# A fused attention, gated-layer and routed-expert kernel: the root's chain on another engine, values loaded earlier, and several pieces of work emitted in another order

## The chip, the cores and the metric

The kernel runs on one core of one Trainium2 chip. A core has a matmul engine (TensorE, "PE" in the rows; its weight loads are listed apart as "PEld"), VectorE ("DVE"), ScalarE ("ACT"), GpSimd ("POOL") and SyncE ("SP"), which issues most of the DMAs. Each engine works through its own list of instructions in order; semaphores make one engine wait for another. SBUF is the working memory, PSUM the memory into which TensorE writes (eight banks of 128 x 512 words of 32 bits). The metric is the device time of one execution in microseconds (us); a run's number is the median of several executions.

## The reference

Three layers follow each other. All inputs are 32-bit floats.

```python
# 1. attention with a sigmoid in place of the softmax: 4 batches, 12 heads, 448 tokens, 64 wide
scores = scale * (q @ k.T) - log(S)
attn_out = sigmoid(scores) @ v                     # laid side by side: x is 1792 x 768
# 2. a gated layer
xn = x / sqrt(mean(x * x) + 1e-6) * rms_g
g, val = xn @ w_gate, xn @ w_val                   # 768 -> 1536
x = (g * sigmoid(g) * val) @ w_out                 # 1536 -> 768
# 3. one of 8 experts for each token
e = argmax(x @ w_gate2); p = softmax(x @ w_gate2)[e]
out = p * (relu(x @ w1[e]) @ w2[e])                # 768 -> 1024 -> 768
```

## The kernel before

The program is one straight list per engine. Python generators emit it: one step emits a piece for each engine, and what one step emits stands in the engines' lists behind what the step before emitted. `later(n, f)` puts a piece off by n ticks.

**Attention.** The 12 heads of a batch make 6 pairs, so there are 24 pairs u over the 4 batches. A pair takes 3.5 steps on the average (two pairs share the rest of 64 tokens), 21 steps a batch (`QS`), 84 in all. Step t issues the scores of its part (`quarters`, L736, PSUM tiles `two`), the weighted sums of the part two steps back (`weighted`, L753, PSUM tiles `one`), and the sigmoid (`weights`, L742, on ScalarE). At a pair's first part SyncE loads the queries and keys of pair u + 2 (`load_pair`, tile `rqk`) and the values of pair u + 1 (`load_v`, tile `rv`). When a pair is summed up, ScalarE copies one PSUM bank, VectorE adds the other (L781), ScalarE squares, VectorE adds the squares to the batch's sum `ss` (L791).

**Beside the attention.** `normalise(b)` starts in the sixth step after batch b's last one: TensorE sums `ss` over the partitions (`pm`, L821), VectorE makes a first estimate of 1 / root (L825 to L833), then a chain of 12 small instructions (three Newton turns, L836 to L839, tiles `ta` and `ya`) refines it; ScalarE spreads it (`yb`, L843), TensorE turns it (`pr`, L847), and six VectorE instructions scale x (L852). One batch after another, the fourth within the gated layer. `conv` (`narrow`, L216 to L229) puts the gated layer's weights together from two halves of 64-bit words on VectorE and stores them to DRAM; SyncE loads the next words. The table `x_at` says in which step the operands of the first seven products are made (`x_sum` L332 and L335, `x_hi` L319, `x_lo` L323).

**Gated layer.** Two batches make a half p. Seven products stand for eight in each of 12 column groups n; `slot(p, n, k)` issues one product, nine matmuls, because each operand is a high and a low part and three of their four products are kept (`three`, L310 to L312). `window(p, n, k)` emits what ScalarE and VectorE do beside it. `abc` holds two sets of three PSUM banks that the column groups take in turn; `dup` (L369) copies one bank into another.

**Output.** `output(p)` has 6 output chunks of 8 turns. The list `pys` gives the bank of a sum. Beside the first turns stand the last window of the gated part (`window(p, KF, m)`) and the high and low parts of what it made (`h_hi`, `h_lo` L457).

**Routing and experts.** `route(b)` is a generator of small steps; half 1's gated part carries those of batches 0 and 1, the expert blocks those of 2 and 3 (`turn(b, steps)`, called by a table of block numbers). Its small matmuls write the bank `mi` (`pl` L592, `pn` L618, `pr` L636 and L637). A batch has 14 expert blocks, 8 of the first weight and 6 of the second. `split_block` makes the high and low part of a block's weight (ScalarE L918, VectorE L919). `mi_bank` takes the next bank of `fixed["mi"]`, which holds one bank, `mi`.

Of the kernel before, what the change touches and what calls it, by code (L numbers as in the profile page):

```python
# [91 lines left out]
def block_kernel(ctx, tc, qkp, v, wg, wv, wo, g, gate, w1, w2, consts, out):  # L92
# [404 lines left out]
    def output(p):  # L497
        pair = {}
        pys = [abc[1][i] for i in (1, 0, 2)]
        logit_bank[2 * p], logit_bank[2 * p + 1] = mi, one[2]  # L500
# [23 lines left out]
        for m in range(8 * KD):  # L524
            oc, q = divmod(m, 8)
            x, g = divmod(q, 4)
            if g == 0:
                pys.append(pys.pop(0))
                py = pys[-1][:, :S]
            h, l = out_w[oc, g // 2]  # L530
            xh, xl = held["hs", g, x, 0][0], held["hs", g, x, 1][0]
            for i in range(HALF):
                c = HALF * g + i
                three(py, (h[:, c % KD, :], l[:, c % KD, :]), (xh[:, i, :], xl[:, i, :]), c == 0, c == KF - 1)
            if oc == KD - 1:
                drop(("hs", g, x, 0))
                drop(("hs", g, x, 1))
            if g == 3:
                later(2, out_copy, py, oc, x)
                if x == 1:  # L540
                    logits(2 * p, oc)
                elif oc > 0:
                    logits(2 * p + 1, oc - 1)
            if m < 2:
                window(p, KF, m)
            if m < 4:
                h_hi(*((3, 0), (1, 1), (2, 1), (3, 1))[m])
            if 0 < m < 5:
                h_lo(*((3, 0), (1, 1), (2, 1), (3, 1))[m - 1])
            if oc + 1 < KD:  # L550
                if q in (0, 3):
                    load_raw(2 * NU * p + 2 * (KF + oc + 1) + q // 3)
                if q >= 4:
                    (hi_o, lo_o)[q % 2](p, oc + 1, q // 2 - 2)
            yield m
# [22 lines left out]
    def route(b):  # L578
# [82 lines left out]
        pf = sm([CT, NC], "pf")  # L661
        nc.vector.tensor_copy(out=pf, in_=ri[:, 1, :])
        for c in range(NC):
            j = b * NC + c
            nc.vector.tensor_scalar(
                out=p1_all[:, j, :],
                in0=const("place", CT),
                scalar1=pf[:, c : c + 1],
                scalar2=const("token1", CT)[:, j : j + 1],
                op0=ALU.is_equal,  # L670
                op1=ALU.mult,
            )
# [35 lines left out]
    def attention():  # L708
# [85 lines left out]
        load_v(0)  # L794
        load_pair(1)
        normal = iter(())
        for t in range(B * QS + LAG):
            if t < B * QS:
                u, c = order[t]
                if c == 0:  # L800
                    load_v(u + 1)
                    load_pair(u + 2)
                quarters(t)
# [13 lines left out]
    def normalise(b):  # L817
# [17 lines left out]
        for _ in range(3):  # L835
            nc.gpsimd.tensor_tensor(out=ta, in0=ya, in1=ya, op=ALU.mult)  # L836
            nc.gpsimd.tensor_tensor(out=ta, in0=ta, in1=va, op=ALU.mult)
            nc.gpsimd.tensor_scalar(out=ta, in0=ta, scalar1=1.5, scalar2=None, op0=ALU.add)
            nc.gpsimd.tensor_tensor(out=ya, in0=ya, in1=ta, op=ALU.mult)  # L839
        for _ in range(4):  # L840
            yield
        yb = keep.tile([CT, NC, 128], F32, tag="xr", name="yb")
        nc.scalar.copy(out=yb, in_=ya.unsqueeze(2).to_broadcast([CT, NC, 128]))  # L843
        yield
        pr = mi[:, :S]
# [284 lines left out]
    def all_slots():  # L1130
# [96 lines left out]
    x_at = {  # L1227
        43: [(x_hi, 0, P1, True)], 44: [(x_lo, 0, P1)], 46: [(x_hi, 0, P2, True)], 47: [(x_lo, 0, P2)],
        64: [(x_sum, 0, P5)], 65: [(x_sum, 0, P7)], 66: [(x_hi, 0, P5, True)], 67: [(x_lo, 0, P5)],
        68: [(x_sum, 0, P6)], 69: [(x_hi, 0, P6, True)], 70: [(x_lo, 0, P6)], 71: [(x_sum, 0, P4)],  # L1230
        72: [(x_hi, 0, P7, True)], 73: [(x_lo, 0, P7)],
    }
    end, done = B * QS, 0
    for n in range(end + LAG):
# [13 lines left out]
        for f, *a in x_at.get(n, ()):  # L1248
            f(*a)
        scaling = n >= QS and n % QS >= 15  # L1250
        if 2 <= n < 70 and not scaling and n not in (44, 47) and (n < 63 or n % 2 == 0):
            next(conv)
            done = (done + 1) % 3
        elif n == 72 and done:
            for _ in range(done, 3):
                next(conv)
# [11 lines left out]
        if n == end:  # L1268
# [3 lines left out]
            abc += [[one[0], *four_banks[:2]], [one[1], *four_banks[2:]]]  # L1272
            slot(0, -1, 4)
        if n == end + 1:
            s_a.close()
            s_x, xd = opened("xd", side="right", reuse_waits="tile")
            s_w, cw = opened("cw", side="right", reuse_waits="tile")
            for r in range(2, 6):
                load_raw(r)
            dup(0)  # L1280
            hi_w(0, 0, P7)
# [75 lines left out]

    fixed.update(mm=abc[0], sc=[abc[1][1], abc[1][0]], av=[abc[1][2], one[2]])
    s_m.close()
# [41 lines left out]
    for u, b, steps in (  # L1401
        (0, 2, 2), (1, 2, 2), (1, 3, 2), (2, 2, 2), (3, 2, 1), (3, 3, 2), (4, 3, 2), (5, 3, 2), (6, 3, 1)
    ):
# [34 lines left out]
    for u in range(B * NB):  # L1438
        if u % NB >= K2 - 1 and u % NB < NB - 1:
            split_block(u + 1)  # L1440
        out_of = block(u)
        tick()
        out_of()
        if (u + 2) % NB < K2:
            split_block(u + 2)
# [73 lines left out]
```

## Time and profile before

| | |
|---|---|
| median of 3 executions | 920.24 us (919.37 to 921.02) |
| the profiled execution, its own time | 919.88 us |
| its span, first to last instruction | 918.0 us, mean granted clock 0.992 |
| TensorE busy | 895.4 us, 98% of the span |
| VectorE busy | 598.3 us, 65% |
| ScalarE busy | 377.1 us, 41% |
| GpSimd busy | 32.0 us, 3% |
| chain that ended last | TensorE 86%, VectorE 7%, DMA 3% of the span |

The span is what the profile sees; about 1.9 us lie around it. TensorE's busy time is so near the span that the time is its work and the places where it waits or runs at half its clock; the views that list these places are the ones to read.

### The profile page before, as it was taken

The page shows a single profiled execution, that of the slowest core. Times are in us where ns is not written, and L with a number is a line of the kernel's source. Part 1 is how long each engine was busy: PE and PEld are TensorE (multiplying, and loading weights), DVE is VectorE, ACT ScalarE, POOL GpSimd, SP SyncE. Part 2 cuts the span into 40 slices and gives each one's busy share as a digit, 9 for nine tenths or more (in the row PEclk, how much of TensorE's full clock was granted, in tenths as well). Part 3 has the DMA queues.
Part 4 walks back from the last instruction along what each step waited for, and adds up shares of the span by engine and source line. Part 5 has one row for each costly group of instructions (what it writes and reads, how often), then busy time and mean ns, then how long its engine had stood idle before and what let it go on. Part 6 is the DMA issues. An engine that isn't in the chain of part 4 may idle for free.

```text
span 918.0 us, 14308 instructions
## 1 busy us (share of the span) xinstructions
PE 895.4 (98%) x5430; PEld 749.4 (82%) x5430; DVE 598.3 (65%) x1074; ACT 377.1 (41%) x605; POOL 32.0 (3%) x59
## 2 busy tenths in 40 slices
PE   8999989999999999999999999999989999999997
PEld 3445435999999889999899998999879988888996
DVE  3777676998988984777897778222576734334454
ACT  6778857444445512354444455121222222222230
POOL 0022040200000000000000000000000000000000
PEclk9999989999999999999999999999999999999999
DMA  8996763354445399841222242547747958749533
GB/s 327 392 347 230 277 215 130 117 202 152 142 138 172 114 330 318 240 114 37 70 69 70 91 150 82 151 131 217 213 112 241 318 181 293 256 149 300 166 61 62
DMA packets 118202, 169.33 MB, mean 184 GB/s; under 512 B 62233, under 2 KB 82585, under 8 KB 118128
## 3 DMA queue, kind: packets, MB, share of 16 engines
q1 hardware_dynamic: 104960, 164.85, 54.5%
q10 hardware_dynamic: 13024, 2.98, 1.7%
q8 instruction: 43, 0.70, 0.3%
q0 software_dynamic: 144, 0.53, 0.3%
q14 instruction: 31, 0.25, 0.1%
HBM read 127.57 MB, written 40.63 MB: 183 GB/s over the span
## 4 chain that ended last, share of the span: by engine, by line
PE 86%; DVE 7%; DMA 3%; POOL 1%; issue 1%; ACT 1%; SPq 0%; DVEq 0%; ACTq 0%; POOLq 0%
PE four L312 13%; PE four L311 13%; PE four L310 13%; PE one L310 12%; PE one L312 12%; PE one L311 12%; PE one L753 4%; PE two L736 4%; DVE m L457 1%; DMA w32d<-wn 1%; PE one L570 1%; DMA w<-in_wg 1%; DMA rv<-in_v 1%; DVE wc L286 1%; PE four L1097 1%
## 5 line engine op out<-in xcount | busy, mean ns | idle before, releaser
L312 PE MATMUL one<-m,wc 128*128 128x448 f32 x282 | 103.2, 366 | 0.0
L310 PE MATMUL one<-m,wc 128*128 128x448 f32 x282 | 102.6, 364 | 0.0
L311 PE MATMUL one<-m,wc 128*128 128x448 f32 x282 | 102.3, 363 | 0.0
L742 ACT ACTIVATE a<-two,logs 128x896 f32<-128x896 f32 x84 | 84.6, 1008 | 30.6 <-PE two L736 28.7
L736 PE MATMUL two<-rqk 64*64 64x448 f32 x672 | 90.4, 557 | 3.8 <-DMA rqk<-in_qkp 3.8
L753 PE MATMUL one<-a,rv 64*64 64x448 f32 x672 | 87.9, 542 | 1.3 <-DMA rv<-in_v 1.2
L312 PE MATMUL four<-m,wc 128*128 128x448 f32 x213 | 78.0, 366 | 0.7 <-DVE wc L286 0.7
L310 PE MATMUL four<-m,wc 128*128 128x448 f32 x213 | 77.6, 364 | 0.0
L311 PE MATMUL four<-m,wc 128*128 128x448 f32 x213 | 77.5, 364 | 0.0
L311 PE MATMUL four<-m,wr 128*128 128x448 f32 x192 | 70.3, 366 | 1.4 <-DVE m L457 1.4
L310 PE MATMUL four<-m,wr 128*128 128x448 f32 x192 | 69.8, 364 | 0.3 <-DVE m L437 0.3
L312 PE MATMUL four<-m,wr 128*128 128x448 f32 x192 | 69.8, 363 | 0.0
L286 DVE TENSOR_TENSOR wc<-raw,wc 128x384 fp32r<-128x384 f32 x115 | 61.6, 549 | 4.5 <-ACT wc L281 4.5
L736 PEld LDWEIGHTS two<-rqk 64*64 64x64 f32 x672 | 30.7, 137 | 39.3 <-issue 21.8
L753 PEld LDWEIGHTS one<-a,rv 64*64 64x64 f32 x672 | 31.0, 135 | 37.7 <-issue 30.7
L311 PEld LDWEIGHTS one<-m,wc 128*128 128x128 f32 x282 | 52.8, 187 | 4.6
L281 ACT CAST wc<-raw 128x384 fp32r<-128x384 f32 x115 | 55.0, 515 | 3.4 <-PE four L311 1.2
L310 PEld LDWEIGHTS one<-m,wc 128*128 128x128 f32 x282 | 52.9, 188 | 4.0
L312 PEld LDWEIGHTS one<-m,wc 128*128 128x128 f32 x282 | 52.9, 188 | 3.8
L918 ACT CAST w2h<-w2r 128x1024 fp32r<-128x1024 f32 x24 | 25.2, 1049 | 59.9 <-PE four L311 30.0
L310 PE MATMUL four<-xc,wr 128*128 128x448 f32 x126 | 47.4, 376 | 0.0
L311 PE MATMUL four<-xc,wr 128*128 128x448 f32 x126 | 46.8, 371 | 0.0
(253 smaller groups left out, 1895.3 us busy)
## 6 DMA issues: line engine op xcount, KB each, us to landing
raw<-w32d SPq DMA_DIRECT2D x70, 384.0 KB, 3.6
w32d<-wn SPq DMA_DIRECT2D x36, 384.0 KB, 3.2
w1r<-in_w SPq DMA_DIRECT2D x24, 512.0 KB, 6.1
w2r<-in_w SPq DMA_DIRECT2D x32, 384.0 KB, 6.4
x2s<-x SPq DMA_DIRECT2D x48, 224.0 KB, 2.0
rqk<-in_qkp SPq DMA_DIRECT2D x23, 448.0 KB, 7.1
w<-in_wg SPq DMA_DIRECT2D x12, 768.0 KB, 7.3
w<-in_wv SPq DMA_DIRECT2D x12, 768.0 KB, 7.4
```

What stands on the lines that cost most here:

```text
L281: nc.scalar.copy(out=h, in_=source(p, n, j).rearrange("p (c k) -> p c k", k=128))
L286: nc.vector.tensor_tensor(out=l, in0=w, in1=f32(h), op=ALU.subtract)
L310: nc.tensor.matmul(p, wh, xh, start=first, stop=False, **kw)
L311: nc.tensor.matmul(p, wh, xl, start=False, stop=False, **kw)
L312: nc.tensor.matmul(p, wl, xh, start=False, stop=last, **kw)
L457: nc.vector.tensor_tensor(out=t, in0=held["h", g, x][0], in1=f32(held["hs", g, x, 0][0]), op=ALU.subtract)
L570: nc.tensor.matmul(logit_bank[b][: 2 * E, :S], gate_2[:, oc, :], x2_t[b, oc][k], start=(oc == 0 and k == 1), stop=(oc == KD - 1 and k == 2),)
L736: nc.tensor.matmul(two[t % 2][o, x, :S], r[head, k : k + D], r[head, :S], start=True, stop=True)
L742: nc.scalar.activation(out=a, in_=two[t % 2][:, :, :S], func=AF.Sigmoid, bias=logs, scale=1.0 / math.sqrt(D))
L753: nc.tensor.matmul(one[2 * y + k][halves[x], :S], v4[halves[i], c, x, :], a[halves[i]], start=(c == first), stop=(c == end))
L918: nc.scalar.copy(out=hv, in_=r)
L1097: nc.tensor.matmul(py[TS * k : TS * k + TS], ht[:, i, TS * j : TS * j + TS], ph2["w2f"][:, c, n * k : n * k + n], start=(c == 0), stop=(c ...
```

## The change

Of the root's chain the 12 GpSimd instructions become 9 on VectorE (one of each three does the addition and a product together); three empty steps fewer stand behind them and one more behind `yb`, so that `pr` is emitted two steps earlier. `x_at` lies four steps earlier throughout. `conv` pauses in other steps. Values are loaded two pairs ahead, the second pair's before the loop. `dup(0)` is emitted a step earlier. The output's first two sums go to banks of the other set, and its last window stands behind the high and low parts instead of ahead of them. `route` gets one more step, two banks take its matmuls in turn, and the first block of a second weight is split a block earlier.

```diff
@@ normalise
-            nc.gpsimd.tensor_tensor(out=ta, in0=ya, in1=ya, op=ALU.mult)
-            nc.gpsimd.tensor_tensor(out=ta, in0=ta, in1=va, op=ALU.mult)
-            nc.gpsimd.tensor_scalar(out=ta, in0=ta, scalar1=1.5, scalar2=None, op0=ALU.add)
-            nc.gpsimd.tensor_tensor(out=ya, in0=ya, in1=ta, op=ALU.mult)
-        for _ in range(4):
-            yield
+            nc.vector.tensor_tensor(out=ta, in0=ya, in1=ya, op=ALU.mult)
+            nc.vector.tensor_tensor(out=ta, in0=ta, in1=va, op=ALU.mult)
+            nc.vector.scalar_tensor_tensor(out=ya, in0=ta, scalar=1.5, in1=ya, op0=ALU.add, op1=ALU.mult)
+        yield
         yb = keep.tile([CT, NC, 128], F32, tag="xr", name="yb")
         nc.scalar.copy(out=yb, in_=ya.unsqueeze(2).to_broadcast([CT, NC, 128]))
+        yield
         yield
@@ attention
         load_pair(1)
+        load_v(1)
...
                 if c == 0:
-                    load_v(u + 1)
+                    load_v(u + 2)
                     load_pair(u + 2)
@@ the attention's loop
-        43: [(x_hi, 0, P1, True)], 44: [(x_lo, 0, P1)], 46: [(x_hi, 0, P2, True)], 47: [(x_lo, 0, P2)],
+        39: [(x_hi, 0, P1, True)], 40: [(x_lo, 0, P1)], 42: [(x_hi, 0, P2, True)], 43: [(x_lo, 0, P2)],
...
-        scaling = n >= QS and n % QS >= 15
-        if 2 <= n < 70 and not scaling and n not in (44, 47) and (n < 63 or n % 2 == 0):
+        scaling = n >= QS and 10 <= n % QS < 16
+        if 2 <= n < 70 and not scaling and n not in (40, 43) and (n < 60 or n % 2 == 0):
...
             slot(0, -1, 4)
+            dup(0)
         if n == end + 1:
...
-            dup(0)
             hi_w(0, 0, P7)
@@ output
-        pys = [abc[1][i] for i in (1, 0, 2)]
+        pys = [abc[0][1], abc[0][2]] + 4 * abc[1]
...
-                pys.append(pys.pop(0))
-                py = pys[-1][:, :S]
+                py = pys.pop(0)[:, :S]
...
-            if m < 2:
-                window(p, KF, m)
             if m < 4:
                 h_hi(*((3, 0), (1, 1), (2, 1), (3, 1))[m])
             if 0 < m < 5:
                 h_lo(*((3, 0), (1, 1), (2, 1), (3, 1))[m - 1])
+            if m < 2:
+                window(p, KF, m)
@@ route
         nc.vector.tensor_copy(out=pf, in_=ri[:, 1, :])
+        yield
         for c in range(NC):
@@ behind output(1)
-    fixed.update(mm=abc[0], sc=[abc[1][1], abc[1][0]], av=[abc[1][2], one[2]])
+    fixed.update(mi=[mi, abc[1][2]], mm=abc[0], sc=[abc[1][1], abc[1][0]], av=[abc[1][2], one[2]])
...
-        (0, 2, 2), (1, 2, 2), (1, 3, 2), (2, 2, 2), (3, 2, 1), (3, 3, 2), (4, 3, 2), (5, 3, 2), (6, 3, 1)
+        (0, 2, 2), (1, 2, 2), (1, 3, 2), (2, 2, 2), (3, 2, 1), (3, 3, 2), (4, 2, 1), (4, 3, 2), (5, 3, 2), (6, 3, 1), (7, 3, 1)
...
-        if u % NB >= K2 - 1 and u % NB < NB - 1:
+        if u % NB >= K2 and u % NB < NB - 1:
             split_block(u + 1)
...
-        if (u + 2) % NB < K2:
+        if (u + 2) % NB <= K2:
             split_block(u + 2)
```

SyncE's list at the program's start, before (`rqk` a pair's queries and keys, the first in two pieces, `rv` its values, `w` words for `conv`):

```order
L698 DMA rqk<-in_qkp 128x576
L698 DMA rqk<-in_qkp 128x320
L705 DMA rv<-in_v 128x512
L698 DMA rqk<-in_qkp 128x896
L705 DMA rv<-in_v 128x512
L698 DMA rqk<-in_qkp 128x896
L207 DMA w_154<-in_wg 128x1536
```

The same place now:

```order
L698 DMA rqk<-in_qkp 128x576
L698 DMA rqk<-in_qkp 128x320
L705 DMA rv<-in_v 128x512
L698 DMA rqk<-in_qkp 128x896
L705 DMA rv<-in_v 128x512 x2
L698 DMA rqk<-in_qkp 128x896
L207 DMA w_156<-in_wg 128x1536
```

One load of values more stands ahead of the third pair's queries and keys, and so ahead of every later load of them; each load of values comes one pair earlier.

VectorE's list around the third batch's root, before, from the first `x_sum` on (L332, L323 and L319 are pieces of `x_at`, `wn` of `conv`, L781 and L791 of the attention; the last L791 is what `pm` waits for, L825 reads `pm`):

```order
L332 TENSOR_TENSOR m<-m 128x1344
L224 SCALAR_TENSOR_TENSOR wn<-w_947,wn 128x768
L781 TENSOR_TENSOR m<-one_133,m 128x448
L332 TENSOR_TENSOR m<-m 128x1344
L319 CAST m<-m 128x1344
L216 TENSOR_SCALAR wn<-w_1000 128x768
L791 TENSOR_TENSOR ss<-ss,sq 128x448
L323 TENSOR_TENSOR m<-m 128x1344
L825 TENSOR_SCALAR va<-one_134 112x4
```

The same place now; ahead of these rows, since the first `x_sum`, stand L332, a `wn` of L224, L332, L781 and L319:

```order
L216 TENSOR_SCALAR wn<-w_945 128x768
L323 TENSOR_TENSOR m<-m 128x1344
L791 TENSOR_TENSOR ss<-ss,sq 128x448
L335 SCALAR_TENSOR_TENSOR m<-m 128x1344
L220 SCALAR_TENSOR_TENSOR wn<-w_945,wn 128x768
L781 TENSOR_TENSOR m<-one_133,m 128x448
L319 CAST m<-m 128x1344
L323 TENSOR_TENSOR m<-m 128x1344
L224 SCALAR_TENSOR_TENSOR wn<-w_945,wn 128x768
L791 TENSOR_TENSOR ss<-ss,sq 128x448
L335 SCALAR_TENSOR_TENSOR m<-m 128x1344
L826 TENSOR_SCALAR va<-one_134 112x4
```

From the first `x_sum` to the last L791 there were 7 instructions and now there are 15.

VectorE's list in the fourth expert block, before (L934 and L919 belong to the block itself; L654 on to `r_pf`, `p_all` and `ck_all` are batch 2's ranks, L595 on are batch 3's choice):

```order
L934 SCALAR_TENSOR_TENSOR hl<-one_131,hh 128x448
L919 TENSOR_TENSOR wr<-w1r,wr 128x768
L654 TENSOR_TENSOR r_rk<-one_134,oh_all 112x32
L656 TENSOR_REDUCE r_rr<-r_rk 112x4
L657 COPY acc<-acc 112x8
L659 CAST r_ri<-r_rr 112x4
L660 TENSOR_SCALAR r_ri<-r_ri 112x4
L662 CAST r_pf<-r_ri 112x4
L665 TENSOR_SCALAR p_all<-cst,r_pf 112x128 x4
L673 TENSOR_TENSOR r_rr<-r_rr,r_pf 112x4
```

The same place now:

```order
L934 SCALAR_TENSOR_TENSOR hl<-one_131,hh 128x448
L919 TENSOR_TENSOR wr<-w1r,wr 128x768
L653 TENSOR_TENSOR r_rk<-one_134,oh_all 112x32
L655 TENSOR_REDUCE r_rr<-r_rk 112x4
L656 COPY acc<-acc 112x8
L658 CAST r_ri<-r_rr 112x4
L659 TENSOR_SCALAR r_ri<-r_ri 112x4
L661 CAST r_pf<-r_ri 112x4
L594 COPY r_lg<-four_1470 112x32
L596 TENSOR_REDUCE r_mx<-r_lg 112x4
```

`p_all` and what follows it moved behind batch 3's choice and the next block's own two instructions; batch 3's `r_lg` now reads a bank of its own (`four_1470`), where `r_rk` and `r_lg` both read `one_134` before.

## Rows read from the trace of the kernel before

**Rows 1.** TensorE's waits: engine, line, waited for: total us, times, longest us

```profile
PE one L847 <- ACT yb L843: 4.0, 1, 4.0
...
PE one L592 <- DVE r_rk L654: 2.5, 1, 2.5
PE four L311 <- DVE m L457: 1.4, 2, 1.0
PE one L753 <- DMA rv<-in_v: 1.2, 1, 1.2
PE one L310 <- ACT four L369: 1.1, 1, 1.1
PE four L312 <- DVE w2l L919: 1.0, 1, 1.0
PE four L312 <- DVE wc L286: 0.7, 1, 0.7
```

**Rows 2.** Stretches: length, PE, PEld, DVE, ACT, POOL busy (count), clock, DMA, GB/s

```profile
10.00:60.00 50.00, 48.69 (x498) 22.28 (x494) 33.99 (x53) 38.20 (x50) 5.46 (x12) 1.00 1.01 384
129.36:136.19 6.83, 6.47 (x32) 3.32 (x36) 1.31 (x3) 3.29 (x5) 0.00 (x0) 0.50 0.92 286
160.00:200.00 40.00, 40.00 (x207) 37.23 (x206) 38.46 (x72) 18.08 (x38) 4.76 (x12) 1.00 0.41 143
300.00:330.00 30.00, 28.71 (x140) 25.22 (x139) 29.83 (x36) 13.53 (x17) 0.00 (x0) 1.00 0.54 177
667.48:678.40 10.92, 10.39 (x50) 9.48 (x50) 7.11 (x36) 1.95 (x5) 0.00 (x0) 0.84 0.33 62
668.67:672.08 3.41, 3.41 (x11) 3.02 (x11) 2.74 (x15) 0.23 (x1) 0.00 (x0) 0.50 0.61 83
```

**Rows 3.** DMA issues from 10 to 60 us: number, KB each, median us to landing

```profile
rv<-in_v SPq DMA_DIRECT2D x8, 256.0 KB, 7.3
```

**Rows 4.** Waits of TensorE's weight loads, same columns as rows 1

```profile
PEld two L736 <- DMA rqk<-in_qkp: 5.1, 5, 3.8
```

**Rows 5.** TensorE around 115 to 130 us: start, us, engine, line, operation, tiles [idle before]

```profile
115.58 0.95 PE L821 MATMUL one<-ones,ss 128*112 128x1 f32 x8 [0.15 <-DVE ss L791]
...
123.28 0.93 PE L753 MATMUL one<-a,rv 64*64 64x448 f32 x8
...
124.78 0.93 PE L753 MATMUL one<-a,rv 64*64 64x448 f32 x8
129.72 0.55 PE L847 MATMUL one<-cst,yb 112*128 112x112 f32 x1 [4.01 <-ACT yb L843]
```

**Rows 6.** VectorE from 102 to 118 us, same columns as rows 5

```profile
102.81 0.62 DVE L791 TENSOR_TENSOR ss<-ss,sq 128x448 f32<-128x448 f32 x1 [1.26 <-ACT sq L790]
...
110.81 0.95 DVE L224 SCALAR_TENSOR_TENSOR wn<-w,wn 128x768 int32<-128x768 int32 x1
111.68 0.62 DVE L781 TENSOR_TENSOR m<-one,m 128x448 f32<-128x448 f32 x1
...
113.68 0.85 DVE L319 CAST m<-m 128x1344 fp32r<-128x1344 f32 x1
114.44 0.55 DVE L216 TENSOR_SCALAR wn<-w 128x768 int32<-128x768 int32 x1
114.91 0.62 DVE L791 TENSOR_TENSOR ss<-ss,sq 128x448 f32<-128x448 f32 x1
115.45 1.55 DVE L323 TENSOR_TENSOR m<-m 128x1344 fp32r<-128x1344 f32 x1
116.92 0.15 DVE L825 TENSOR_SCALAR va<-one 112x4 f32<-112x4 f32 x1
...
117.38 0.17 DVE L830 TENSOR_SCALAR ya<-ta 112x4 int32<-112x4 int32 x1
```

**Rows 7.** GpSimd's chain of the third root, its first and last of 12

```profile
117.69 2.31 POOL L836 TENSOR_TENSOR ta<-ya 112x4 f32<-112x4 f32 x1 [26.84 <-DVE va L833]
...
128.82 0.20 POOL L839 TENSOR_TENSOR ya<-ya,ta 112x4 f32<-112x4 f32 x1
```

More of the change, by code (lines that the diff above doesn't have):

```diff
@@ L1227, in block_kernel @@
     x_at = {
-        43: [(x_hi, 0, P1, True)], 44: [(x_lo, 0, P1)], 46: [(x_hi, 0, P2, True)], 47: [(x_lo, 0, P2)],
-        64: [(x_sum, 0, P5)], 65: [(x_sum, 0, P7)], 66: [(x_hi, 0, P5, True)], 67: [(x_lo, 0, P5)],
-        68: [(x_sum, 0, P6)], 69: [(x_hi, 0, P6, True)], 70: [(x_lo, 0, P6)], 71: [(x_sum, 0, P4)],
-        72: [(x_hi, 0, P7, True)], 73: [(x_lo, 0, P7)],
+        39: [(x_hi, 0, P1, True)], 40: [(x_lo, 0, P1)], 42: [(x_hi, 0, P2, True)], 43: [(x_lo, 0, P2)],
+        60: [(x_sum, 0, P5)], 61: [(x_sum, 0, P7)], 62: [(x_hi, 0, P5, True)], 63: [(x_lo, 0, P5)],
+        64: [(x_sum, 0, P6)], 65: [(x_hi, 0, P6, True)], 66: [(x_lo, 0, P6)], 67: [(x_sum, 0, P4)],
+        68: [(x_hi, 0, P7, True)], 69: [(x_lo, 0, P7)],
     }
```

## Prediction

> **What bounds the kernel now.** I read the page first: TensorE is busy for nearly the whole span and carries the chain that ended last. So only two things can change the time by much, TensorE's waits and the stretches in which it runs at half its clock. I then read the waits of TensorE [rows 1] and, where a wait stood, the windows around it [rows 2]. The reader is to see in rows 1 that four waits stand where the change works: 4.0 us for the third root's `yb`, 2.5 us for batch 2's ranks, 1.2 us for values, 1.1 us for `dup`, and behind them 1.4 us in two waits for `h_lo`, 1.0 us for the first split of a second weight and 0.7 us for a low part that stands behind routing. [...]
>
> The sum below is made against the profiled execution, 919.88 us (918.0 us of span and 1.9 us around it), which is 0.36 us under the median of 920.24. I add the 0.36 at the end. This measurement tells about 0.2% from no change, 1.8 us.
>
> **Values two pairs ahead.** From 10 to 60 us the DMA engines are full (share 1.01, 384 GB/s) [rows 2], and a load of values lands 7.3 us after its issue [rows 3], nearly the length of the pair and two steps that it has. With a pair more of lead (3.5 steps of 1.5 us, the distance of equal rows in [rows 5]) it comes in time, and the 1.2 us go. But nothing is loaded less. One load of 256 KB more stands ahead of every load of queries and keys, 0.7 us at 384 GB/s, and those are wanted two steps sooner than the values. They have no slack: besides the start's 3.8 us, four more waits for them stand before the weight loads, 1.3 us together [rows 4]. As TensorE no longer waits for values, it comes to them 1.2 us sooner, and they come 0.7 us later. Bounds: if all is hidden after all, the 1.2 us are gained; if the 1.2 us are only handed on and each of the four pairs pays its 0.7 us anew, 2.8 are lost. I take the waits as handed on, with the delay paid once and a part of it again: **+1.0** (from -1.2 to +2.8).
>
> **The third root.** What goes: the wait of 4.01 us before L847 [rows 5] and the 3.2 us at half clock behind it, -7.2. GpSimd's twelve instructions took from 117.69 to 129.02 us [rows 7]; nine on VectorE, each hanging on the one before, take nine times the spacing of such small ones, 0.23 us (two of them from 116.92 to 117.38 us) [rows 6], 2.1 us. [...]
>
> What comes: `x_at` is four steps earlier, but `pm` is not, so VectorE has more to do ahead of the sum of squares that `pm` waits for. The first `x_sum` now stands behind the L791 that the trace has at 102.81 us, which frees VectorE at 103.35. From there to the last L791, by the distances in rows 6: five of L332, L323 and L335 at 1.47 us (one size, the row is L323's), two of L319 at 0.76, three `wn` of 0.87, one L216 of 0.47, four of L781 and L791 at 0.54; together 14.1 us, so 117.5 us. Before, `pm` was wanted at 115.4 (it began at 115.58 after 0.15 us of waiting) [rows 5]. A new wait of 2.1 us, and the 0.15 are in it: +2.0.
>
> Is `yb` in time then? `pm` runs from 117.55 to 118.45. VectorE does L335 (1.47, to 119.0), reads `pm` and makes the first estimate (four small ones, 0.6), L319, L216 and L781 (1.8), the nine (2.1): 123.5; the spread copy on ScalarE adds some 0.6: 124.1. `pr` is wanted four steps behind `pm`, 6.0 us, at 124.45. Nothing is left over but 0.3 us; I take no wait (0 to 1.0). Together **-5.2** (from -7.2 to -4.0, the clock apart).
>
> **The fourth root** lies in the gated part, where VectorE is busy 38.46 of 40 us [rows 2] and feeds TensorE with low parts. GpSimd's chain lay beside it for nothing. Now 2.1 us stand in VectorE's list, and 1.5 us were free in 40: between 0 and 2.1, nearer the upper end: **+1.5**. At the first two roots VectorE has room (33.99 of 50 us busy) [rows 2]: 0.
>
> **`dup(0)`** goes ahead of ScalarE's other work, and the 1.1 us of L310 go [rows 1]: **-1.1** (-1.1 to 0).
>
> **The first half's output.** The wait for `h_lo` was once 1.0 us, the other time 0.4 [rows 1]. VectorE is busy 29.83 of 30 us there [rows 2], and nothing is taken from its list; it is put in another order. Earlier low parts are paid with a later window, and a later low part of the output's first copies, which the logits wait for. Free banks don't help an engine that has no time: **0** (-1.3 to +1.2). In the second half's output VectorE has room, as no `conv` runs: the 0.4 us go, **-0.4**. `route`'s new step takes `p_all` from ahead of the low part that L312 waited for: **-0.7**.
>
> **Routing in the expert blocks.** With two banks, `pl` of batch 3 need not wait until `r_rk` has read `pr` of batch 2: 2.5 us and the 1.7 us of half clock go. The split goes ahead of routing: 1.0 us goes. But VectorE's list still holds both batches' small work, and TensorE meets it at its next small matmul. Unhindered, TensorE would reach `pr` of batch 3 after 10.39 less 1.7 = 8.7 us of its own work; VectorE starts 2.5 us late and has 7.1 us to do in that stretch, and the gaps in it are waits for the blocks' ends [rows 2]. So 0.9 us to 2.5 us come back; I take +1.7, spread over two small matmuls, at full clock. Together 1.7 - 2.5 - 1.7 - 1.0 = **-3.5** (-5.2 to -2.7).
>
> **Sum.** 1.0 - 5.2 + 1.5 - 1.1 + 0 - 0.4 - 0.7 - 3.5 = -8.4. 919.88 - 8.4 = 911.5, and on the median 911.8 us.
>
> **Rivals.** *The clock falls at the new wait.* The new wait for `pm` (2.1 us, and behind it 0.9 us of the tiny `pm`) is like the one before L592 (2.5 us and tiny matmuls), behind which the clock fell [rows 1, 2]. Against it: it is shorter, and the waits of 1.0 to 1.2 us show no lower level in rows 2's full stretches. [...] The price is one such stretch, 1.7 us, to two, 3.2: 913.5 to 915.0 us. *The third root stays late.* If VectorE is much later than its rows sum up to, `yb` is waited for as before: 4.0 us and a fall of the clock, 1.7 to 3.2: 917.5 to 919.0, little or no gain. For it: VectorE's list has eight instructions more ahead of `pm`. Against it: they fill time in which it idled, as the 1.26 us before the first of rows 6. *Slower: queries and keys.* In the first 60 us, if the loads share the engines so that the queries and keys wait for the whole of the values issued ahead of them, the four pairs without slack [rows 4] may each hold TensorE as long as 2.5 us, and the clock falls behind two of them as it did behind L592. Then in place of +1.0 stand 10.0 - 1.2 + 3.4 = +12.2: 923.0 us. From 9.4 us lost in this stretch on, the kernel is slower than before. Against it: 0.7 us is all that a load of values takes at the stretch's rate.
>
> **How the numbers follow.** Forecast 0.57; clock falls at `pm` 0.25; the root stays late 0.08; slower by the loads 0.05; the rest, 0.05, is a mishap of another kind that eats half the gain or more. The forecast's own range is 909.0 to 914.5: the bounds of the loads, the fourth root, the first output and routing, none of which hang together. With the second case at the upper end and the third left out: 908.5 to 916.8 us. Faster by over 0.2% means under 918.4 us: forecast, clock, half of the third case and most of the rest, 0.90; within 0.2%: 0.05; slower: 0.05.
>
> **What would show it.** In the waits of TensorE, `yb`, values, `r_rk`, `dup` and the split of the second weight should be gone. New ones should be: L736 for `rqk` before 50 us (over 2 us together), `pm` (L822) for `ss` at about 2.1 us, a low part (L286) behind the fourth root, and `pn` or `pr` of batch 3. Granted clock 1.00 from 10 us to the end's last stretch; a row of 0.50 behind `pm` is the first rival. If `yb` is still waited for over 1 us, my queue of VectorE is wrong; if the waits for `rqk` are under 1 us, the loads had slack; if the output's waits fall by over 1 us, VectorE was not what bound it there.

## The result and the profile after

The changed kernel took 910.15 us, median of 4 executions (909.20 to 910.93), the kernel before 920.63 on the same chip: ratio 0.9887 (0.987 to 0.9904). Six more executions beside the later experiments (e6 below) took 913.13 us (910.14 to 915.62), ratio 0.9931 (0.9904 to 0.9958). The median of all ten is 910.75, between 910.58 and 910.93; the prediction was 911.8. How one kernel comes to lie at 910 and at 913 us is the main thing that the experiments found.

The profiled execution took 910.14 us, with a span of 908.3. First TensorE's waits, which answer to [rows 1]; the columns are the same:

```profile
PE two L736 <- DMA rqk<-in_qkp: 4.7, 2, 3.7
PE one L822 <- DVE ss L791: 2.2, 1, 2.2
PE four L635 <- DVE oh_all L628: 1.0, 1, 1.0
PE one L569 <- DVE x L508: 0.7, 1, 0.7
PE four L311 <- DVE m L457: 0.6, 2, 0.4
PE one L312 <- DVE wc L286: 0.3, 1, 0.3
PE four L636 <- DVE acc L632: 0.3, 1, 0.3
PE one L847 <- ACT m L780: 0.3, 1, 0.3
```

The waits for `yb` (4.0), `r_rk` (2.5), values (1.2), `dup` (1.1), the first split of a second weight (1.0) and `route`'s low part (0.7) are gone. New are `pm` for `ss` (L822, 2.2), the queries before 50 us (4.7 less the start's 3.7) and batch 3's `pr` (L635 and L636, 1.3 together). The logits' wait (L569) and a shorter one for `h_lo` (L311, L457) stand in the first half's output.

The same stretches as in [rows 2], moved to where the work now lies (length; PE, PEld, DVE, ACT, POOL busy; clock; DMA share; GB/s):

```profile
10.00:60.00 50.00, 48.98 (x504) 22.50 (x500) 34.41 (x61) 38.51 (x50) 0.00 (x0) 1.00 1.00 390
114.47:117.25 2.78, 0.54 (x8) 0.00 (x0) 2.78 (x4) 1.79 (x3) 0.00 (x0) 1.00 0.00 0
117.25:124.66 7.41, 7.12 (x72) 3.20 (x72) 6.52 (x19) 4.48 (x7) 0.00 (x0) 1.00 0.95 355
160.00:200.00 40.00, 39.38 (x198) 35.92 (x197) 38.02 (x73) 18.96 (x40) 0.00 (x0) 1.00 0.51 176
300.00:330.00 30.00, 28.73 (x140) 25.28 (x140) 28.73 (x36) 9.93 (x13) 0.00 (x0) 1.00 0.69 229
663.45:672.00 8.55, 6.96 (x35) 5.65 (x34) 7.17 (x29) 2.65 (x5) 0.00 (x0) 1.00 0.21 18
```

Row 2 is the wait for `pm`: VectorE is busy through all of it, so it is VectorE's list that is late. No row shows 0.50; in this execution the clock stays at 1.00 behind that wait (117.25 to 124.66 us).

VectorE's chain now (start, us, engine, line, operation, tiles), to be read beside [rows 7]:

```profile
118.59 0.15 DVE L826 TENSOR_SCALAR va<-one 112x4 f32<-112x4 f32 x1
...
120.90 0.15 DVE L837 TENSOR_TENSOR ta<-ya 112x4 f32<-112x4 f32 x1
121.08 0.16 DVE L838 TENSOR_TENSOR ta<-ta,va 112x4 f32<-112x4 f32 x1
...
122.47 0.16 DVE L839 SCALAR_TENSOR_TENSOR ya<-ta,ya 112x4 f32<-112x4 f32 x1
```

Nine instructions, 120.90 to 122.63 us, 0.20 apart: 1.7 us where GpSimd's twelve took 11.3.

Where the gain arises is read from the starts of the same matmuls in the two traces (my table, us):

| matmul | before | after | difference | what lies since the row above |
|---|---|---|---|---|
| step 68, first score | 113.75 | 113.33 | -0.42 | loads |
| step 80, first score | 141.48 | 136.31 | -5.17 | third root, -4.75 |
| first gated product | 148.34 | 144.08 | -4.26 | last pair, +0.91 |
| 75th L310 | 197.39 | 193.04 | -4.35 | `dup` and fourth root, -0.09 |
| 297th L310 | 334.88 | 330.54 | -4.34 | first output, 0 |
| 482nd L310 | 453.49 | 448.21 | -5.28 | `p_all`, -0.94 |
| 667th L310 | 567.84 | 561.87 | -5.97 | second output, -0.69 |
| 852nd L310 | 693.95 | 684.55 | -9.40 | routing, -3.43 |
| end of the span | 917.99 | 908.35 | -9.64 | end, -0.24 |

### The profile page after: what moved, and what is told of

Its sections match the earlier page's. It is cut to its first block, busy times and chain, and to the rows that moved or that the text cites. A ratio compares the mean times of both kernels' runs of the same rounds, so it can differ in the third digit from the quotient of the medians.

```text
span 908.3 us, 14255 instructions
## 1 busy us (share of the span) xinstructions
PE 891.8 (98%) x5430; PEld 745.3 (82%) x5430; DVE 602.0 (66%) x1110; ACT 376.4 (41%) x605; POOL 4.7 (1%) x11
## 4 chain that ended last, share of the span: by engine, by line
PE 88%; DVE 8%; DMA 1%; issue 1%; ACT 1%; SPq 0%; ACTq 0%; DVEq 0%
PE four L310 13%; PE four L311 13%; PE four L312 13%; PE one L310 12%; PE one L311 12%; PE one L312 12%; PE two L736 6%; PE one L753 5%; DMA rqk<-in_qkp 1%; DVE m L457 1%; PE one L569 1%; DVE wc L286 1%; PE four L1097 1%; PE four L1073 1%; DVE wn L224 1%
## 5 line engine op out<-in xcount | busy, mean ns | idle before, releaser
L310 PE MATMUL one<-m,wc 128*128 128x448 f32 x282 | 102.8, 365 | 0.3 <-ACT c L396 0.3
L311 PE MATMUL one<-m,wc 128*128 128x448 f32 x282 | 102.8, 365 | 0.0
L736 PE MATMUL two<-rqk 64*64 64x448 f32 x672 | 89.2, 552 | 4.7 <-DMA rqk<-in_qkp 4.7
L753 PE MATMUL one<-a,rv 64*64 64x448 f32 x672 | 86.6, 537 | 0.0
L310 PE MATMUL four<-m,wc 128*128 128x448 f32 x213 | 77.9, 366 | 0.0
L311 PE MATMUL four<-m,wc 128*128 128x448 f32 x213 | 77.7, 365 | 0.0
L311 PE MATMUL four<-m,wr 128*128 128x448 f32 x192 | 70.4, 367 | 0.6 <-DVE m L457 0.6
L310 PE MATMUL four<-m,wr 128*128 128x448 f32 x192 | 69.5, 362 | 0.0
L736 PEld LDWEIGHTS two<-rqk 64*64 64x64 f32 x672 | 29.0, 135 | 41.6 <-issue 24.7
L753 PEld LDWEIGHTS one<-a,rv 64*64 64x64 f32 x672 | 30.0, 133 | 35.4 <-issue 33.5
L310 PEld LDWEIGHTS one<-m,wc 128*128 128x128 f32 x282 | 52.9, 188 | 5.0 <-ACT c L396 0.7
L311 PEld LDWEIGHTS one<-m,wc 128*128 128x128 f32 x282 | 52.9, 188 | 4.1
L310 PE MATMUL four<-xc,wr 128*128 128x448 f32 x126 | 46.7, 371 | 0.0
L311 PE MATMUL four<-xc,wr 128*128 128x448 f32 x126 | 46.2, 367 | 0.0
```

Of the source, the lines that this page charges most:

```text
L310: nc.tensor.matmul(p, wh, xh, start=first, stop=False, **kw)
L311: nc.tensor.matmul(p, wh, xl, start=False, stop=False, **kw)
L736: nc.tensor.matmul(two[t % 2][o, x, :S], r[head, k : k + D], r[head, :S], start=True, stop=True)
L753: nc.tensor.matmul(one[2 * y + k][halves[x], :S], v4[halves[i], c, x, :], a[halves[i]], start=(c == first), stop=(c == end))
```

## Experiments

Ratios are to the kernel before, run beside them on the same chip. The experiments stand on three chips (e1 to e4, e5 to e8, e9 to e12), on which the kernel before took 919.86, 919.51 and 919.88 us; the changed kernel was run again on the second only. "Ahead" and "late" are read as in the table. The mean granted clock is known of every execution, the trace of one.

**The root and the values, by parts (e1, e2, e3, e5).** e1 puts only the chain on VectorE, in the kernel before, with `pr` two steps earlier and `conv`'s pauses moved to fit:

```diff
-            nc.gpsimd.tensor_tensor(out=ta, in0=ya, in1=ya, op=ALU.mult)
...
+            nc.vector.tensor_tensor(out=ta, in0=ya, in1=ya, op=ALU.mult)
+            nc.vector.tensor_tensor(out=ta, in0=ta, in1=va, op=ALU.mult)
+            nc.vector.scalar_tensor_tensor(out=ya, in0=ta, scalar=1.5, in1=ya, op0=ALU.add, op1=ALU.mult)
-        for _ in range(4):
-            yield
+        yield
...
-        scaling = n >= QS and n % QS >= 15
+        scaling = n >= QS and 10 <= n % QS < 16
```

> The kernel before with the nine VectorE instructions in place of GpSimd's twelve and pr two steps earlier; x_at stays where it was. My theory: the engine of the chain alone removes what the third root cost. Then pm waits as before (0.2 us), L847 waits 1 to 2 us for yb in place of 4.0, no granted clock of 0.50 stands behind it (3.2 us), and the fourth root pays about 1.1 us in VectorE's full stretch: -2.5 - 3.2 + 1.1 = -4.6, so 4 to 5 us under the kernel before (ratio 0.9945 to 0.9957). Rival: VectorE is too full between pm and the chain, and it is the earlier x_at that makes room. Then L847 still waits 3 us or more, the clock still falls, and the time is 0 to 1 us from before.

920.05 us against 919.86, ratio 0.9994 (0.9981 to 1.0007): no gain. Yet its trace (918.42 us, among its shorter executions) shows what the theory wanted: the turn of the root (L847, here L846) waits 1.4 us, the clock doesn't fall there (mean 0.997), and TensorE is 6.34 us ahead at step 80. The 1.4 us are not for `yb`, which ScalarE had made by 122.11 us, but for a copy of a sum that stands behind it in ScalarE's list (L780). TensorE then loses more than half of its lead again (its own rows, with [idle before <- for what]):

```profile
123.49 0.92 PE L846 MATMUL one<-cst,yb 112*128 112x112 f32 x6 [1.39 <-ACT m L780]
...
135.14 0.92 PE L736 MATMUL two<-rqk 64*64 64x448 f32 x4
137.69 0.59 PE L736 MATMUL two<-rqk 64*64 64x448 f32 x2 [1.63 <-DMA rqk<-in_qkp]
...
142.29 0.59 PE L753 MATMUL one<-a,rv 64*64 64x448 f32 x2 [0.57 <-DMA rv<-in_v]
```

The last pair's queries and values did not come sooner because TensorE did: it waited 1.63 and 0.57 us for them. At the first gated product 2.90 us are left, and the fourth root in VectorE's full stretch takes 1.16 of them.

e2 adds the earlier `x_at` and conv's other pauses:

```diff
@@ e1, and
-        64: [(x_sum, 0, P5)], 65: [(x_sum, 0, P7)], 66: [(x_hi, 0, P5, True)], 67: [(x_lo, 0, P5)],
+        60: [(x_sum, 0, P5)], 61: [(x_sum, 0, P7)], 62: [(x_hi, 0, P5, True)], 63: [(x_lo, 0, P5)],
...          the other entries of x_at four steps earlier too
```

> The kernel before with the whole change of the root: chain, steps and the earlier x_at. My theory: the earlier x_at only trades one wait for another: pm waits 2.2 us, L847 0.3 us, no half clock at 129 us, and the fourth root pays 1.1 us: +2.1 - 3.7 - 3.2 + 1.1 = -3.7, so 3.2 to 4.5 us under the kernel before (ratio 0.995 to 0.9965), within 1 us of the chain alone. Rival: the earlier x_at is part of the gain: 2 us or more under the chain alone. Second rival, the clock falls at the new wait: a row of 0.50 behind pm and 1.7 to 3.2 us more.

919.99 us, ratio 1.0005 (0.999 to 1.0021): again none, and within 1 us of e1, so the earlier `x_at` is no part of a gain. The second rival held in its trace: the clock fell behind the wait for `pm` (stretch, length, PE busy, clock, DMA share, GB/s):

```profile
114.41:117.22 2.81, 0.53 (x8) 0.97 0.00 0
117.07:123.90 6.83, 6.68 (x36) 0.50 0.92 319
```

6.68 us of work at 0.50 cost an estimated 3.3 us, half of it; by the same estimate the 6.47 us behind `yb` [rows 2] cost 3.2.

e3 is the values alone:

```diff
+        load_v(1)
...
-                    load_v(u + 1)
+                    load_v(u + 2)
```

> The kernel before with the values loaded two pairs ahead and nothing else. My theory from the two traces: behind the first pairs the queue holds values and queries in turn as before, so the queries and keys land when they did (42.87 before, 42.55 with the whole change); the wait for rv before L753 goes and one for rqk of 1.0 us before L736 stands in its place: -0.8 to 0 us, ratio 0.999 to 1.000. Rival (the term of the prediction): each load of values that stands ahead delays the queries by 0.7 us, paid once or twice: +0.5 to +1.5 us. Second rival: all is hidden, -1.2 us and no wait for rqk behind the start.

919.87 us, ratio 0.9994 (0.9978 to 1.0011), and in its trace the wait for `rqk` in place of that for values, 0.81 us ahead at the end of the attention. That is no sign of the values: e4, which leaves them alone, is 0.77 us ahead there. The time cannot choose between -0.8 and +0.5: all lie within the interval. What the loads themselves did is told with e9.

e5 is e2 and e3 together:

```diff
@@ e2 and e3
```

> The kernel before with the whole change of the root and the values two pairs ahead, nothing else. What it is to tell: alone, the root's change gave no gain (919.99 against 919.86) though TensorE was 5 to 6 us early at step 80; behind it stood waits for the last pair's queries and for its values (in the chain-alone trace a gap of 2.16 us at 135.5 and one of 1.10 at 141.2). My theory: the two parts are worth more together, as the last load of values no longer stands in that queue: gaps at the end of the attention under 0.6 us each, TensorE 3 to 3.5 us ahead of the kernel before in the gated part, so 915.5 to 917.5 us where the clock stays up behind pm. Rival: the parts add up, 0 to -0.5 us, 919.4 to 920. Second rival: the clock falls behind pm as often as it did behind yb; then half or more of the executions show a mean clock of 0.994 or less and the time is 918 to 920.

918.99 us, ratio 0.999 (0.9972 to 1.0008). In its trace the clock stayed up behind `pm` (mean 0.997), and TensorE was 3.97 us ahead in the gated part (3 to 3.5 were expected). But of its 12 executions only four had a mean clock of 0.997 (915.27 to 918.99), and five 0.994 or less (919.22 to 920.83). So neither theory nor rival holds for all: the gain is there in some executions and spent on the clock in others. That the two parts are worth more together isn't shown.

**Routing alone (e4)**, in the kernel before:

```diff
+        yield            # ahead of p_all
-    fixed.update(mm=abc[0], ...
+    fixed.update(mi=[mi, abc[1][2]], mm=abc[0], ...
-        ... (3, 3, 2), (4, 3, 2), (5, 3, 2), (6, 3, 1)
+        ... (3, 3, 2), (4, 2, 1), (4, 3, 2), (5, 3, 2), (6, 3, 1), (7, 3, 1)
-        if u % NB >= K2 - 1 and u % NB < NB - 1:
+        if u % NB >= K2 and u % NB < NB - 1:
-        if (u + 2) % NB < K2:
+        if (u + 2) % NB <= K2:
```

> The kernel before with the routing part alone: two banks in turn, route's new step, the earlier split. My theory: the wait for r_rk, the half clock behind it and the split's wait go (-2.5 - 1.7 - 1.0), p_all's step gives 0.9 us near 447 us, and 1.5 to 2.0 us come back at pn and pr of batch 3: -4.1 to -4.6 us, ratio 0.995 to 0.9956. Rival: the wait moves whole to pr of batch 3, with the fall of the clock behind it: -1.9 us (the split and p_all alone), ratio 0.998.

915.31 us, ratio 0.9944 (0.9921 to 0.9966): the theory's size, and the one part that shows in the time by itself. Its trace has a fall of the clock all the same, 3.41 us at 0.50 (674.46 to 677.87 us) behind `pr` of batch 3 (waits of 1.1 and 0.3 us); there it gained 1.9 us, where the changed kernel's trace, without the fall, has 3.43.

**The changed kernel again (e6)**, without an edit:

> The changed kernel itself, more executions of it on the chip of the next ones. My theory: whether the clock falls behind a wait of some 2 us differs from execution to execution of one kernel; so most of its executions lie at 909 to 911 us with a mean clock of 0.997 or more, and some (1 to 5 of 12) 1.7 to 3.3 us higher, at 0.994 to 0.996. Ratio 0.987 to 0.991. Rival: the fall is fixed by the wait's length, then all executions have one clock and lie within 1.5 us.

Median 913.13 us, as above. The ten executions of the one kernel: mean clock 0.998 in five, at 909.20 to 910.58 us; 0.996 or 0.995 in the others, at 910.93 to 915.62. The theory's spread holds; its share was too low, with four of these six. The trace of e6 shows what the first one didn't:

```profile
115.06:117.85 2.79, 0.52 (x9) 1.00 0.00 0
120.00:123.41 3.41, 3.41 (x24) 0.50 1.01 379
666.00:672.96 6.96, 5.59 (x29) 1.00 0.07 2
672.96:676.37 3.41, 3.41 (x11) 0.50 0.07 2
```

The wait for `pm` is the same (2.3 us for 2.2), the clock falls behind it and again behind `pr` of batch 3. Against the first trace TensorE loses 1.36 and 1.43 us in these two places; the rest of the 3.2 us between the spans is loads in the first 60 us, the last pair and the end.

**Fewer and more pieces ahead of `pm` (e7, e8)**, both from the changed kernel:

```diff
@@ e7
-        64: [(x_sum, 0, P6)], 65: [(x_hi, 0, P6, True)], 66: [(x_lo, 0, P6)], 67: [(x_sum, 0, P4)],
-        68: [(x_hi, 0, P7, True)], 69: [(x_lo, 0, P7)],
+        64: [(x_sum, 0, P6)], 69: [(x_hi, 0, P6, True)], 70: [(x_lo, 0, P6)], 71: [(x_sum, 0, P4)],
+        72: [(x_hi, 0, P7, True)], 73: [(x_lo, 0, P7)],
@@ e8
+        58: [(x_sum, 0, P5)], 59: [(x_sum, 0, P7)], 60: [(x_hi, 0, P5, True)], 61: [(x_lo, 0, P5)],
+        62: [(x_sum, 0, P6)], 63: [(x_hi, 0, P6, True)], 64: [(x_lo, 0, P6)], 65: [(x_sum, 0, P4)],
+        66: [(x_hi, 0, P7, True)], 67: [(x_lo, 0, P7)],
```

> The changed kernel with the last five entries of x_at put behind the third root (steps 69 to 73, the first five stay at 60 to 64). My theory: the 2.2 us that TensorE waits at pm are the sum of the pieces that the earlier x_at put ahead of the sum of squares; with 3.7 us of them behind it, pm and yb (0.3) are waited for under 0.3 us each: -2 to -3.5 us against the changed kernel, and no fall of the clock at 117 us in any execution. Rival: VectorE is full there and the pieces that are put behind make yb late: L847 waits 2 us or more, gain 0 to 0.5. Second rival: the low parts come too late for the first products, a new wait at L311 or L312 after 144 us of 1 us or more.

909.88 us, ratio 0.9909 (0.9886 to 0.9933), against 913.13 for the changed kernel beside it. TensorE runs through both places:

```profile
113.46 0.93 PE L753 MATMUL one<-a,rv 64*64 64x448 f32 x8
114.32 0.95 PE L822 MATMUL one<-ones,ss 128*112 128x1 f32 x8
115.20 0.98 PE L736 MATMUL two<-rqk 64*64 64x448 f32 x8
...
120.51 0.93 PE L753 MATMUL one<-a,rv 64*64 64x448 f32 x8
121.37 0.81 PE L847 MATMUL one<-cst,yb 112*128 112x112 f32 x5
```

Both rivals fell: the wait for `pm` is the earlier `x_at`, and the pieces have room behind it. In the trace TensorE needs 2.67 us less than in the changed kernel from step 68 to step 80, and loses 1.03 of them again at the last pair, where queries are waited for. Five of its six executions have a mean clock of 0.998, against five of the changed kernel's ten; these five have a median of 909.36 us, the changed kernel's five 910.14. So most of the 3.2 us between the two medians is the clock, which may in part be chance.

> The changed kernel with all pieces of x_at from step 60 on two steps earlier, so that two more of them (2.2 us) stand ahead of the sum of squares. My theory: pm waits longer, 3.0 to 4.4 us in place of 2.2, yb is not waited for, and the clock falls behind pm in most executions (3.3 us for 6.83 us at the lower level, 1.7 for 3.41): +0.5 to +2 us by the waits and 2 to 4.5 with the clock, against the changed kernel. Rival: VectorE has idle time ahead that takes the pieces in, pm waits 2.2 us as before and the time is the same within 0.5 us.

913.57 us, ratio 0.9939 (0.9921 to 0.9957). The wait is 2.7 us against e6's 2.3, not 3.0 to 4.4, but the eight weighted sums just ahead of it took 1.46 us in place of 0.93, so 0.9 of the 2.2 us came through to TensorE. VectorE's idle time took about as much in: from 100 us to its last L791 it was idle for 0.15 us, in the changed kernel's first trace for 0.99. The clock fell in its trace (mean 0.994), and nine of its twelve executions have 0.996 or less; with four of six in e6 that is no clear difference, and the time is the rival's, 0.4 us from the changed kernel.

**The wait filled with work (e10)**, from the changed kernel:

```diff
+        if b == 2:
+            for _ in range(3):
+                nc.tensor.matmul(mi[:, :S], ones, cst[:, :S], start=True, stop=True)
         pm = mi[:CT, :NC]
```

> The changed kernel with three matmuls of 128 x 448 ahead of the third root's sum over the partitions; nothing reads what they write. TensorE thus works through most of the 2.2 us in which it waited for the sum of squares. My theory: the wait's length and the clock are two costs. The sum of squares comes as late as before (pm starts within 0.4 us of the changed kernel's 117.25 us), but the clock does not fall there in any execution: mean clocks of 0.996 or more in at least 10 of 12, and the median 0 to 2 us under the changed kernel's 913.1 on that chip (909.5 to 912). Rival: the fall has another cause than TensorE's idle time; then 0.994 to 0.995 are seen as often as in the changed kernel (2 of 6) and the times spread as before, 910 to 915.6.

```profile
114.98 2.52 PE L822 MATMUL one<-cst,ones 128*128 128x448 f32 x6
117.34 0.90 PE L825 MATMUL one<-ones,ss 128*112 128x1 f32 x8
```

The trace lists each of the three matmuls as two. `pm` starts where it did (117.34 against 117.25), so nothing of the wait's length is saved, as expected. All six executions have a mean clock of 0.996 or more, and the median is 910.93 us (909.33 to 913.55). That is what the theory said, but it doesn't show it: three of the six have 0.996 and so most likely a fall somewhere, only two of the changed kernel's ten have 0.995, and the median of those ten is 910.75. Whether work put into the wait keeps the clock up stays open.

**Parts taken back out (e9, e11).**

```diff
@@ e9
-        load_v(1)
-                    load_v(u + 2)
+                    load_v(u + 1)
@@ e11
-        pys = [abc[0][1], abc[0][2]] + 4 * abc[1]
+        pys = [abc[1][i] for i in (1, 0, 2)]
...          window(p, KF, m) ahead of h_hi and h_lo
```

> The changed kernel with the values loaded one pair ahead again. My theory: near 40 us a wait for values takes the place of the one for queries (within 0.3 us), and at the last pair the load of its values stands behind the stores again: a gap for rv of 0.6 to 1.1 us near 142 us and 0.5 us more for rqk at 136 us; TensorE 1.0 to 1.6 us later than in the changed kernel at the first gated product (144.08), the ratio to before 0.988 to 0.995 as the clock falls or not. Rival (the prediction's term): the loads cost 1.0 us, so without them TensorE is 1 us earlier there.

912.27 us, ratio 0.992 (0.9895 to 0.9946). In its trace TensorE waited for no load near 40 us and was 1.37 us earlier there than in the changed kernel, as the rival has it; a fall of the clock at 117.4 us (mean 0.994) took that again. At the last pair two weighted sums started 0.60 us behind the ones before them, where 0.37 is usual, but from step 80 to the first gated product it lost only 0.13 us more than the changed kernel, not 1.0 to 1.6: the theory fell there. One trace doesn't decide the rest, since these waits vary: at step 40 the five traces with values one pair ahead lie at 67.59 to 69.28 us, the eight with two pairs (e12 apart, which issues the queries first) at 68.03 to 69.80, means 68.6 and 69.0. The loads are clearer: the sixth pair's queries and keys landed at 29.88 to 30.33 us in the five and at 30.45 to 31.68 in the eight, 0.8 us later in the mean.

> The changed kernel with the outputs' first banks and the order of window and low parts as before. My theory: in the first half's output VectorE is full, so the waits only change place (h_lo 1.0 us at 311 us and a bank at 305 in place of 0.4, 0.4 and 0.6 for the logits): within 0.2 us at the first gated product of half 1; in the second half's output 0.7 us more (a wait for h_lo). Together +0.4 to +0.9 us, not to be told from the changed kernel in the time, but in the trace. Rival: the order also shortens VectorE's list or the logits, +1.5 us or more at the first output alone.

912.63 us, ratio 0.9924 (0.9899 to 0.9949), in the trace 0.0 us at the first output and 0.66 at the second: the theory in both places. The waits only change place in the first half:

```profile
PE four L311 <- DVE m L457: 1.4, 2, 1.0
...
PE four L310 <- DVE m L437: 0.3, 1, 0.3
```

**A better version (e12)**: e7, the queries issued ahead of the values, and batch 3's `pr` a block later.

```diff
@@ e7, and
-                    load_v(u + 2)
                     load_pair(u + 2)
+                    load_v(u + 2)
-        ... (4, 3, 2), (5, 3, 2), (6, 3, 1), (7, 3, 1)
+        ... (4, 3, 2), (6, 3, 2), (7, 3, 1), (8, 3, 1)
```

> The changed kernel with x_at split as in the run before (five pieces behind the third root), queries and keys issued ahead of the values, and batch 3's ranks (pr and what follows) one expert block later. My theory: no wait at pm (2.2 us) and none for oh_all before L635 (1.1 and 0.3 with its gaps, 1.5 to 2 us), queries 0.7 us earlier near 41 us: 3.5 to 5 us under the changed kernel, 1 to 2 us under the split alone (909.88), mean clock 0.998 in nearly every execution as no wait over 1 us is left behind the start: 905.5 to 908.5, ratio 0.986 to 0.989 on that chip. Rival: with the ranks later, the slots' small work meets VectorE's blocks and a new wait of 1 us or more stands at 675 to 700 us; then the time is that of the split alone.

906.72 us (903.88 to 907.67), ratio 0.9855 (0.9829 to 0.9881): each of its six executions lies under each of the changed kernel's ten. Of TensorE's waits behind the start one of over 1 us is left, for queries, which going first did not cure (5.1 less 3.7):

```profile
PE two L736 <- DMA rqk<-in_qkp: 5.1, 2, 3.7
PE one L569 <- DVE x L508: 1.0, 2, 0.6
PE four L311 <- DVE m L457: 0.6, 2, 0.4
PE four L312 <- DVE w2l L919: 0.4, 1, 0.4
```

The waits at `pr` are gone, and no new one of 1 us stands there: from the second output to the 852nd L310 the trace needs 2.0 us less than the changed kernel's. The mean clock is 0.998 to 1.000 in all six.

## Why the prediction was right, and where it was not

The time came within its range, and its mechanisms were there: every wait that was to go went, and the new ones came where it put them. By its steps:

- **Values: +1.0, measured -0.4 in the trace and +0.4 over thirteen.** The wait was handed on to the queries, 1.0 us for 1.2. The load that ends it landed at 42.55 us where it had landed at 42.87, which looks as if "0.7 us later" had failed; but two traces mislead here. Over thirteen the sixth pair's queries and keys land 0.8 us later (e9), so the delay was there, and e3's theory, by which they land when they did, is the one that falls. What was too large is what TensorE pays for it. From 8 to 68 us the five traces with values one pair ahead wait 0 to 1.2 us for values, 0.6 in the mean, and the trace that the prediction read had the longest of these; the eight with two pairs wait 0 to 2.0 us for queries, 1.1 in the mean. The waits of "over 2 us together" that the prediction wanted to see before 50 us were 1.0 in the changed kernel's first trace. Of the four waits that it took for a lack of slack [rows 4], two lie in the first 9 us. At the last pair the part is worth -0.1 us (e9) to -0.6 (e1's wait).
- **Third root: -5.2, measured -4.75.** `pm` waited 2.2 us for 2.1. The nine took 1.7 us for 2.1; `yb` was ready at 123.28, 0.8 us before my 124.1. The 0.3 us before L847 are not for `yb` but for a copy of a sum by ScalarE (L780) that must leave the bank first. What the sum left out is the last pair: TensorE comes five microseconds early, its weight loads wait 0.7 us for queries, and 0.91 us go back. With the fourth root that makes 2.1 us given back, against 1.5 us of waits saved (4.0 for 2.2 and 0.3): apart from the clock's 3.2 us, the root's part is worth nothing.
- **Fourth root: +1.5, measured +1.16** (e5, which has it without the new `dup`). **`dup`: -1.1, measured -1.25**, the difference between -0.09 and 1.16. **Outputs: 0 and -0.4, measured 0 and -0.69. `p_all`: -0.7, measured -0.94.**
- **Routing: -3.5, measured -3.43** with the clock up. 1.3 us of waits came back at `pr`.
- **The clock.** This is the step that was wrong in kind. The sum took -3.2 and -1.7 us for falls that go, as properties of the kernel, and the first rival priced a new one at 1.7 to 3.2 us, with a chance of 0.25 for the whole kernel. The 3.2 and 1.7 us stand in no run as such: they are estimates, half of TensorE's busy time in the two stretches of 0.50 of [rows 2] (6.47 and 3.41 us). In the trace before, groups of eight matmuls started 1.5 us apart at 0.50 and 0.75 apart at 1.00 (131.70 to 138.47 us, L736 and L753); a fall of 3.41 us cost 1.36 and 1.43 us in e6. The runs show a property of the execution: by their mean clocks (0.995 or 0.996 against 0.998) five of ten had a fall, their median is 913.44 against 910.14, and the rival's 913.5 is what those took. My 911.8 lies between the two, so that it held the median of the ten was in part luck. The kernel before varies too: of its 65 executions beside the experiments 58 have a mean clock of 0.994 or less (917.46 to 923.82 us) and seven 0.996 (914.80 to 917.68). Those seven can't have had both falls of [rows 2], as 10.24 us at half clock make 0.994 at most. That a fall differs from execution to execution at a wait in the middle of the kernel was not to be seen in the one trace that the prediction read; the two traces of the changed kernel, with waits of 2.2 and 2.3 us at the same place, one without a fall (1.00) and one with (3.41 us at 0.50), show it.
- **The root stays late** and **slower by the loads** did not occur in any of the eight traces that hold the whole change or most of it.

Why the root's change alone (e1) shows nothing in the median follows in part. Its executions have a higher mean clock (0.994 to 0.998, the kernel before 0.991 to 0.996), so falls did go. But at a like clock it is slower: its seven executions at 0.996 to 0.998 took 918.26 to 920.36 us, the seven of the kernel before at 0.996 took 914.80 to 917.68. Its trace has the reason: 2.6 us less of waiting at the root, 3.4 us lost again at the last pair and 1.16 at the fourth root, 2.0 us more without the clock. Open is what its longer executions lose besides; the one trace lies 1.6 us under the median.

## What to carry to other kernels

Behind one and the same wait of the matmul engine (2.2 and 2.3 us) the clock fell in some executions and not in others, for 1.4 us more (the changed kernel's first trace and e6). So take several executions and their mean clocks before a sum over one trace is believed, of the kernel before as well, and compare at a like clock. Work moved ahead on a full VectorE (busy 2.78 of 2.78 us) made the sum that was queued there 2.2 us late; put such work behind the instruction that the bottleneck engine waits for next (e7, 2.67 us at that place). A gain ahead of a stream of loads lasted here only as far as the loads were early too (e1, 3.4 of 6.3 us lost).

## What the runs showed of the hardware

How often the granted clock fell to 0.50 behind the same wait, over the fourteen traces (before, after and the twelve experiments), the stretch of 0.50 at the end of every trace left out:

| TensorE's wait | length, us | traces with it | with a fall |
|---|---|---|---|
| `yb` (L847) | 4.0 | 3 | 3, each 6.83 us |
| `r_rk` (L592) | 2.5 | 5 | 4, each 3.41 us |
| `ss` (`pm`) | 2.2 to 2.7 | 7 | 4, one 6.83, three 3.41 us |
| `oh_all`, `acc` (`pr` of batch 3) | 1.1 and 0.3 | 8 | 4, each 3.41 us |
| the root's turn in e1 (L846, for a copy by L780) | 1.4 | 1 | 0 |

But for `yb`, it fell behind the waits of one place in some traces and not in others; three traces are few, and seven executions of the kernel before can't have had both its falls. The falls are not independent: five traces hold both the wait for `ss` and those for `pr` (after, e6, e8, e9, e11), and in them the clock fell behind both or behind neither. No fall stood at 117 us where the wait was gone (e7, e12) or filled (e10), nor in three traces that had it (after, e5, e11). A fall of 3.41 us cost 1.36 and 1.43 us (e6).

Small instructions of 112 x 4 elements that hang on each other followed at 0.20 us on VectorE, each 0.16 us long (120.90 to 122.63 us of the changed kernel's trace): nine took 1.7 us.
